# Moving the z loads of a fused FFT convolution and soft MoE to GpSimd, in long runs and two row blocks

## The chip, the cores and the metric

The kernel runs on one core of one Trainium2 chip. The time is the device time of one execution, in microseconds (us). The medians quoted are of all runs of a kernel. Most of these runs are of the state "fast"; one of the changed kernel's four and two of e3_fourbuf's four are labelled slow. A ratio is the mean time of one kernel's fast runs over that of the other's fast runs in the same rounds, so it is not quite the ratio of the medians quoted; a ratio carries a 95% interval. The experiments ran on five chips, where the median of the kernel before was 988 to 995 us, so experiments of different chips are best compared by their ratios.

## The reference

```python
# x: (8, 5696, 128), h: (5696, 128)
Xf, Hf = rfft(x, n=2*S, axis=1), rfft(h, n=2*S, axis=0)
y = irfft(Xf * Hf, n=2*S, axis=1)[:, :S]          # a causal long convolution
x = y.reshape(45568, 128)
logits = x @ phi                                   # 32 slots, 4 for each of 8 experts
d = softmax(logits, axis=0); slot_in = d.T @ x     # over all tokens
slot_out = relu(slot_in @ w1) @ w2                 # per expert
out = softmax(logits, axis=1) @ slot_out
```

## The kernel before

The convolution is a transform in two factors (90 and 64), all as matmuls, and runs as a pipeline over 72 "steps" of 8 to a batch. Stage A transforms columns and stores f to DRAM; stage B loads f, multiplies by the spectrum of h, transforms back and stores z to DRAM; stage C loads z, does the last transform, the logits and both softmaxes. Stage C takes two steps for a *pair* of chunks, and there are four pairs to a batch, 32 in all. The parts that matter:

```python
    def load_z(c):                       # one chunk: 90 rows, 8 KB each
        b, j = divmod(c, NJ)
        t_ = zring.pop(0); zring.append(t_)
        w_ = 2 * CH * 2 * D
        nc.sync.dma_start(out=t_[Z0:Z0 + N1, ...],            # Z0 = 20
                          in_=zd[b].rearrange(...)[:, j * w_:(j + 1) * w_])
    ...
    def stage_c1(T, between):
        za, zb = zs.pop(2 * T), zs.pop(2 * T + 1)
        ...                              # 16 matmuls that read za and zb, PSUM copies, sums
        def after():                     # four GpSimd operations on y, 5.3 us
            ...
    # z store of stage B: three buffers
        st = bpool.tile([P, 2, 2 * D], F32, name="zst", tag="zst", bufs=3)
        nc.scalar.activation(st[:, 0:n, :], bz[:, 0:n, 0:2 * D], AF.Copy)
        nc.sync.dma_start(out=zd[g - 1][...], in_=st[:, 0:n])
    # the loop over steps
        if pair(1 - 2 * ahead) is not None:      # ahead = 1 in the main part, 2 in the tail
            load_pair(pair(1 - 2 * ahead))       # first thing in the step before use
        ...                                      # stages A, B, C
        if U is not None:
            softmax(U)                           # ends with a GpSimd multiply
```

In the main part there is room for one pair of z only: the load of the next pair must wait for the 16 matmuls that read this one, and the next 16 must wait for that load.

Of the kernel before, what the change touches and what calls it, by code (L numbers as in the profile page):

```python
# [10 lines left out]
F32 = mybir.dt.float32  # L11
# [3 lines left out]
PSUM = bass.MemoryType.PSUM  # L15


def transform_tables(S, N1, N2, CH, Z0, X0, F0, F1):












    N, R1, HALF, P = N1 * N2, S // N2, N2 // 2, 2 * N2
    k1 = np.arange(N1)
    alpha = np.pi * (k1 + 0.5) / N1
    m1 = np.arange(R1) - (N1 - 1) / 2
    a1 = np.outer(m1, alpha)
    s1 = np.stack([np.cos(a1), -np.sin(a1), -np.cos(a1)], 1)
    a0 = np.outer(alpha, np.arange(N1 // 2) + 0.5)
    i1 = np.stack([np.cos(a0), -np.sin(a0), -np.cos(a0)], 1)
    NP = N1 // 2
    part = s1  # L40
    s1 = np.zeros((P, 3, P))
    for a, p in enumerate((F0, F1)):
        s1[X0:X0 + R1, :, p:p + NP] = part[:, :, a * NP:(a + 1) * NP]
    i1 = np.pad(i1[np.arange(N1).reshape(2, N1 // 2).T.reshape(-1)],
                [(Z0, P - N1 - Z0), (0, 0), (0, N2 - N1 // 2)])
    k2 = np.arange(N2)
    omega = np.pi * (k1[:, None] + 2 * N1 * k2[None] + 0.5) / N
    m2 = np.arange(HALF) - (N2 - 1) / 2
    a2 = m2[None, :, None] * omega[:, None, :]
    w = np.concatenate([np.cos(a2), np.sin(a2)], 1)  # L50
    back = np.arange(N2).reshape(2, HALF // CH, CH).transpose(1, 0, 2).reshape(-1)
    NU = (NP + 1) // 2
    turn = (N1 - 1) / 2 * alpha[:, None] + (N2 - 1) / 2 * omega
    wq = np.zeros((2, N2, NP, N2))
    vq = np.zeros((2, N2, NU, 2, N2))
    tn = np.zeros((2, N2, 2, NU, 2))
    for a in range(2):
        wq[a] = w[a * NP:(a + 1) * NP].transpose(1, 0, 2)
        for q in range(NP):
            vq[q % 2, :, q // 2, a] = w[a * NP + q][back].T  # L60
            tn[q % 2, :, 0, q // 2, a] = np.cos(turn[a * NP + q]) / N
            tn[q % 2, :, 1, q // 2, a] = np.sin(turn[a * NP + q]) / N
    wq, vq, tn = [t.reshape(P, *t.shape[2:]) for t in (wq, vq, tn)]
    return [np.ascontiguousarray(t, dtype=np.float32) for t in (s1, i1, wq, vq, tn)]
# [3 lines left out]
def kernel(  # L68
# [24 lines left out]
    nc = tc.nc  # L93
    P = 128
    B, S, D = x.shape
# [4 lines left out]
    N1, N2 = 90, 64  # L100
    R1, HALF, NP = S // N2, N2 // 2, N1 // 2
    CH = 4
    NJ = HALF // CH
# [4 lines left out]
    HP = P // 2  # L108
    NQ = NJ // 2
    assert S == R1 * N2 and R1 == N1 - 1 and D == P and CH == Q == 4  # L110
    SPLIT = R1 // 16 * 16
    Z0, X0, F0, F1 = 20, 20, 6, 82
    ctx.enter_context(tc.manual_schedule())

    t_s1, t_i1, t_w, t_v, t_turn = [
        nc.inline_tensor(t, f"tab_{n}").ap()
        for n, t in zip(("s1", "i1", "w", "v", "turn"), transform_tables(S, N1, N2, CH, Z0, X0, F0, F1))]
    fd = [nc.dram_tensor(f"f_{g}", (2, N2, NP, 2, D), F32, kind="Internal").ap() for g in range(B + 1)]
    zd = [nc.dram_tensor(f"z_{b}", (NP, 2 * N2, 2, D), F32, kind="Internal").ap() for b in range(B)]
    cd = nc.dram_tensor("c_t", (P, B * NQ, Q, 2, MH), F32, kind="Internal").ap()  # L120
# [7 lines left out]
    i1 = const.tile([P, 3, HP], F32, name="i1")  # L128
    acc = const.tile([P, D + 1], F32, name="acc")
    NT = B * NQ  # L130
# [12 lines left out]
    ypool = work.enter_context(tc.tile_pool(name="ypool", bufs=1))  # L143
# [7 lines left out]
    bpool = front.enter_context(tc.tile_pool(name="bpool", bufs=1))  # L151

    s1 = apool.tile([P, 3, P], F32, name="s1", tag="s1", bufs=1)
    wt = fconst.tile([P, NP, HP], F32, name="wt")
    vt = fconst.tile([P, NU, 2, HP], F32, name="vt")
    turn = fconst.tile([P, 2, NU, 2], F32, name="turn")
# [110 lines left out]
    def stage_b2(u):  # L267
        g, i = divmod(u, NU)
        if g == 0:
            return  # L270
        n = min(2, NP - 2 * i)
        y_ = prods.pop(u)
        bz = bps.tile([P, 2, 512], F32, name="bz", tag="bz")
        for q in range(n):
            r = slice(q * HP, (q + 1) * HP)
            for a in range(2):
                nc.tensor.matmul(bz[a * HP:(a + 1) * HP, q, 0:2 * D], vt[r, i, a, :],  # L277
                                 y_[r, a, :, :].rearrange("p c d -> p (c d)"),
                                 start=True, stop=True)
        st = bpool.tile([P, 2, 2 * D], F32, name="zst", tag="zst", bufs=3)  # L280
        nc.scalar.activation(st[:, 0:n, :], bz[:, 0:n, 0:2 * D], AF.Copy)  # L281
        nc.sync.dma_start(
            out=zd[g - 1][2 * i:2 * i + n, :, :, :].rearrange("q r c d -> r q (c d)"),
            in_=st[:, 0:n, :])
# [2 lines left out]

    zs, ys, Ls, ds = {}, {}, {}, {}
    ybufs = [ypool.tile([P, Q * CH, D + 1], F32, name=f"y{i}") for i in range(2)]
    zring = [ypool.tile([P, 2, CH, 2, D], F32, name=f"zc{i}") for i in range(2)]  # L290
    lt = ypool.tile([P, CH, 2, HP], F32, name="lt")
    dt = ypool.tile([P, CH, 2, HP], F32, name="dt")
    om, op = [ypool.tile([P, CH, D], F32, name=n) for n in ("om", "op")]
    yt = ypool.tile([D, Q * CH, 2, MH], F32, name="yt")
    for t_ in zring:
        nc.vector.memset(t_[:, :, :, :, :], 0.0)
    for t_ in (lt, dt):
        nc.vector.memset(t_[:, :, :, :], 0.0)
    for t_ in ybufs:
        nc.vector.memset(t_[:, :, D:D + 1], 1.0)  # L300

    def load_z(c):
        b, j = divmod(c, NJ)
        t_ = zring.pop(0)
        zring.append(t_)
        w_ = 2 * CH * 2 * D
        nc.sync.dma_start(
            out=t_[Z0:Z0 + N1, :, :, :, :].rearrange("k o n c d -> k (o n c d)"),
            in_=zd[b].rearrange("q (a r) c d -> (q a) (r c d)",
                                a=2)[:, j * w_:(j + 1) * w_])  # L310
        zs[c] = t_

    def load_pair(T):
        if T < NT:
            load_z(2 * T)
            load_z(2 * T + 1)

    def stage_c1(T, between):
        za, zb = zs.pop(2 * T), zs.pop(2 * T + 1)
        y_ = ybufs[T % 2]  # L320

        def part(v, f):
            k = (2 * v + f) * CH
            return y_[:, k:k + CH, 0:D] if f == 0 else y_[:, k + CH - 1:k - 1:-1, 0:D]

        def product(o, tab, q):
            p = bank()
            for h_, t_ in enumerate((za, zb)):
                nc.tensor.matmul(p[h_ * HP:(h_ + 1) * HP, :], i1[:, tab, :], t_[:, o, :, q, :],  # L329
                                 start=True, stop=True)  # L330
            return p[:, :].rearrange("p (n d) -> p n d", d=D)

        def fold_out(even, minus, plus):
            nc.vector.tensor_tensor(out=plus, in0=even, in1=minus, op=AL.add)  # L334
            nc.vector.tensor_tensor(out=minus, in0=even, in1=minus, op=AL.subtract)

        b_, a_ = product(0, 1, 1), product(0, 0, 0)
        nc.scalar.activation(part(0, 0), b_, AF.Copy)  # L338
        fold_out(a_, part(0, 0), part(1, 0))
        between()  # L340
        b_, a_ = product(1, 1, 0), product(1, 2, 1)
        nc.scalar.activation(om[:, :, :], b_, AF.Copy)

        def after():
            fold_out(a_, om[:, :, :], op[:, :, :])
            for v, o_ in ((1, op), (0, om)):
                for part_, sign in ((part(v, 1), AL.subtract), (part(v, 0), AL.add)):
                    nc.gpsimd.tensor_tensor(out=part_, in0=part(v, 0), in1=o_[:, :, :], op=sign)  # L348

        ys[T] = y_  # L350
        return after
# [193 lines left out]
    for t in range(steps):  # L545
        us = list(units(t))

        def pair(lag):
            T, half = divmod(t - LAG_C - lag, 2)
            return T if half == 0 and 0 <= T < NT else None  # L550
# [18 lines left out]
        for tab, src, first, n, k in ((wt, t_w, LAG_B - 2, NP, 2 * PER),  # L569
                                      (vt, t_v, LAG_B + NJ - 2, NU, PER)):  # L570
            p0 = k * (t - first)
            if 0 <= p0 < n:
                v = slice(p0, min(n, p0 + k))
                nc.sync.dma_start(out=tab[:, v], in_=src[:, v])
        if pair(1 - 2 * ahead) is not None:
            load_pair(pair(1 - 2 * ahead))
        if t < NA:
            load_x(t + 3)
            stage_a(t, 0)
# [28 lines left out]
        if U is not None:  # L608
            softmax(U)
            if U == NT - 1:  # L610
                join_quarters()
        if t == NJ:
            prefetch(AHEAD)
        if t == NA:
# [5 lines left out]
        if t == last_front:  # L620
            front.close()
            rings.append(mid.enter_context(tc.tile_pool(name="ps2", bufs=4, space=PSUM)))
            last = work.enter_context(tc.tile_pool(name="last", bufs=1))
            tail["last"] = last
            tail["cT"] = last.tile([P, B, R1, 2 * NJ], F32, name="cT")
            tail["pool"] = cload.enter_context(tc.tile_pool(name="cload", bufs=3))
            w2s = last.tile([P, E, NFC, D], F32, name="w2s")
            for i in range(2):
                t_ = last.tile([P, 2, CH, 2, D], F32, name=f"zd{i}")
                nc.vector.memset(t_[:, :, :, :, :], 0.0)  # L630
                zring.insert(i, t_)
            assert pair(1) is not None
            load_pair(pair(1) + 2)
            ahead = 2
# [19 lines left out]
    p = bank()  # L654
# [127 lines left out]
```

## Time and profile before

| | before |
|---|---|
| median time | 992.21 us (991.51 to 998.82, 4 runs) |
| span of the profiled run | 980.8 us (this execution took 982.5, less than any of the four timed ones) |
| TensorE, VectorE, ScalarE, GpSimd busy | 88, 68, 52, 47% |
| DMA bytes | 272.79 MB, 278 GB/s over the span |
| period of a pair, 285.47 to 710.96 us | 23.6 us (18 periods) |
| ScalarE waiting for z stores, 190 to 800 us | 67.4 us |

The row of periods is the useful one: cut a steady pipeline at the same instruction of each turn, and the differences say more than busy shares. Below, pairs are numbered from 0 by the start of their first product: pair 0 starts at 192.52 us, pair 4 at 285.47, pair 22 at 710.96, pair 31 at 874.77. (The prediction overlooked pair 0 and counts one less.)

### The profile page before, as it was taken

To read this page: it belongs to the slowest core of one execution; us is meant where nothing else is said; L and a number is where in the kernel's file an instruction comes from. 1 tells how busy PE (TensorE), PEld (TensorE's weight loads), DVE (VectorE), ACT (ScalarE), POOL (GpSimd) and SP (SyncE) were. 2 spreads that over 40 slices of the span, in tenths; PEclk is the share of its full clock that TensorE was granted. 3 is DMA by queue.
4 is the path that set the end of the run, shared out by engine and by line. 5 is a ranking of instruction groups with operands and counts; after the bars stand their busy time and mean duration, and the time that the engine had idled before them with its cause. 6 is when DMAs were issued, how large, how long until landed. Compare 5 with 4: busy or idle time off the path is not lost.

```text
span 980.8 us, 20314 instructions
## 1 busy us (share of the span) xinstructions
PE 862.6 (88%) x7220; PEld 403.2 (41%) x7220; DVE 671.7 (68%) x1137; ACT 510.8 (52%) x1051; POOL 462.4 (47%) x427
## 2 busy tenths in 40 slices
PE   6778788899999999999999999999998887875893
PEld 2222233334444444444444444444443333332883
DVE  2034577568888878777878787777788996554542
ACT  3557545445666655556555565555554443443442
POOL 5546532245555555555555555555533432694000
PEclk9979999999999999999999999999999997797875
DMA  7988899899999998998999899989998996853598
GB/s 193 269 260 266 266 324 327 270 312 295 301 294 313 296 299 276 287 303 261 307 289 297 266 298 287 300 261 288 306 279 264 297 285 190 247 174 122 224 406 328
DMA packets 177283, 272.79 MB, mean 278 GB/s; under 512 B 15024, under 2 KB 119728, under 8 KB 171423
## 3 DMA queue, kind: packets, MB, share of 16 engines
q1 hardware_dynamic: 176607, 271.13, 88.7%
q8 instruction: 58, 0.95, 0.4%
q10 hardware_dynamic: 576, 0.36, 0.2%
q14 instruction: 42, 0.34, 0.1%
HBM read 143.04 MB, written 128.39 MB: 277 GB/s over the span
## 4 chain that ended last, share of the span: by engine, by line
PE 55%; DMA 22%; POOL 7%; DVE 6%; issue 3%; ACT 3%; SPq 2%; DVEq 0%; ACTq 0%; POOLq 0%
PE bank L204 19%; PE bank L329 11%; PE bt L237 9%; DMA z<-zst 8%; PE bz L277 6%; DMA zc<-z 5%; POOL y L348 5%; DMA out_dram<-o 4%; DMA gt<-f 3%; PE bank L357 3%; PE bank L442 2%; PE bank L366 2%; PE bank L395 1%; DVE yf L263 1%; DMA f<-fst 1%
## 5 line engine op out<-in xcount | busy, mean ns | idle before, releaser
L204 PE MATMUL bank<-x,s 128*128 128x512 f32 x576 | 287.3, 626 | 9.5 <-POOL x L193 7.9
L193 POOL TENSOR_TENSOR x<-xc 128x512 f32<-128x512 f32 x144 | 183.4, 1275 | 141.0 <-PE bank L204 124.6
L281 ACT ACTIVATE zst<-bz 128x512 f32<-128x512 f32 (+1 forms) x184 | 108.3, 588 | 222.6 <-PE bz L277 138.5
L206 ACT ACTIVATE fst<-bank 128x512 f32<-128x512 f32 x288 | 168.6, 597 | 86.0 <-PE bank L204 69.0
L258 DVE TENSOR_TENSOR pr<-bt,Hr 128x512 f32<-128x512 f32 (+1 forms) x184 | 126.6, 688 | 81.3 <-PE bt L237 77.2
L237 PE MATMUL bt<-gt,wt 64*64 64x256 f32 x1620 | 138.2, 404 | 37.6 <-PE bz L277 9.9
L263 DVE TENSOR_TENSOR yf<-pr,pi 128x512 f32<-128x512 f32 (+1 forms) x184 | 158.1, 859 | 6.4
L204 PEld LDWEIGHTS bank<-x,s 128*128 128x128 f32 x576 | 100.5, 193 | 132.8 <-issue 89.0
L329 PE MATMUL bank<-zc,i 128*64 128x512 f32 x480 | 137.6, 620 | 17.3 <-ACT y L338 11.4
L261 DVE TENSOR_TENSOR pi<-bt,Hi 128x512 f32<-128x512 f32 (+1 forms) x184 | 125.2, 681 | 0.0
L277 PE MATMUL bz<-yf,vt 64*64 64x256 f32 x1440 | 118.1, 382 | 7.0 <-DVE yf L263 4.5
L237 PEld LDWEIGHTS bt<-gt,wt 64*64 64x64 f32 x1620 | 44.4, 132 | 154.7 <-PE bank L204 52.4
L348 POOL TENSOR_TENSOR y<-y,op 128x512 f32<-128x512 f32 x64 | 75.7, 1183 | 59.2 <-DVE op L334 56.6
L348 POOL TENSOR_TENSOR y<-y,om 128x512 f32<-128x512 f32 x64 | 85.4, 1334 | 2.5
L403 POOL MEMSET dt<- 64x8 f32 x32 | 3.4, 107 | 175.8 <-ACT dn L406 115.3
L277 PEld LDWEIGHTS bz<-yf,vt 64*64 64x64 f32 x1440 | 53.4, 132 | 45.0 <-issue 9.5
L357 PE MATMUL bank<-ident,y 109*128 109x109 f32 x512 | 60.7, 266 | 10.5 <-POOL y L348 10.4
L329 PEld LDWEIGHTS bank<-zc,i 128*64 128x64 f32 x480 | 32.5, 138 | 87.3 <-issue 40.5
L359 ACT ACTIVATE yt<-bank 128x360 f32<-128x360 f32 x128 | 53.0, 471 | 29.3 <-PE bank L357 29.2
L248 DVE SCALAR_TENSOR_TENSOR Hr<-bt,turn,ph 128x128 f32<-128x128 f32 (+1 forms) x46 | 16.0, 349 | 76.0 <-ACT ph L246 76.0
L357 PEld LDWEIGHTS bank<-ident,y 109*128 109x128 f32 x512 | 49.6, 143 | 26.4 <-POOL y L348 17.0
L334 DVE TENSOR_TENSOR y<-bank,y 128x512 f32<-128x512 f32 x32 | 22.1, 690 | 44.9 <-ACT y L338 36.8
(95 smaller groups left out, 911.1 us busy)
## 6 DMA issues: line engine op xcount, KB each, us to landing
f<-fst SPq DMA_DIRECT2D x288, 180.0 KB
gt<-f SPq DMA_DIRECT2D x198, 256.0 KB
z<-zst SPq DMA_DIRECT2D x176, 256.0 KB
zc<-z SPq DMA_DIRECT2D x60, 720.0 KB
xc<-in_x_dram SPq DMA_DIRECT2D x64, 320.0 KB
out_dram<-o SPq DMA_DIRECT2D x16, 1024.0 KB
out_dram<-o SPq DMA_DIRECT2D x8, 768.0 KB
c_t<-cst SPq DMA_DIRECT2D x26, 180.0 KB
```

Of the source, the lines that this page charges most:

```text
L193: nc.gpsimd.tensor_tensor(out=y_[:, :, :], in0=t_[:, 0, :, :], in1=t_[:, 1, ::-1, :], op=AL.subtract if comp else AL.add)
L204: nc.tensor.matmul(p[:, :], s1[:, tab[G], :], src[:, :, :].rearrange("p n d -> p (n d)"), start=True, stop=True)
L206: nc.scalar.activation(st[:, :, G, :], p[:, :].rearrange("p (n d) -> p n d", d=D), AF.Copy)
L237: nc.tensor.matmul(bt[q * HP:(q + 1) * HP, a, 0:2 * D], wt[r, 2 * i + q, :], t_[r, q, :, :].rearrange("p c d -> p (c d)"), start=True, sto ...
L258: nc.vector.tensor_tensor(out=pr[r, :, :, :], in0=pv, in1=Hr[r, i, :, :].unsqueeze(2).broadcast_to([n * HP, 2, 2, D]), op=AL.mult)
L261: nc.vector.tensor_tensor(out=pi[r, :, :, :], in0=pv, in1=Hi[r, i, :, :, :], op=AL.mult)
L263: nc.vector.tensor_tensor(out=y_[r, :, :, :], in0=pr[r, :, :, :], in1=pi[r, :, ::-1, :], op=AL.add)
L277: nc.tensor.matmul(bz[a * HP:(a + 1) * HP, q, 0:2 * D], vt[r, i, a, :], y_[r, a, :, :].rearrange("p c d -> p (c d)"), start=True, stop=True)
L281: nc.scalar.activation(st[:, 0:n, :], bz[:, 0:n, 0:2 * D], AF.Copy)
L329: nc.tensor.matmul(p[h_ * HP:(h_ + 1) * HP, :], i1[:, tab, :], t_[:, o, :, q, :], start=True, stop=True)
L348: nc.gpsimd.tensor_tensor(out=part_, in0=part(v, 0), in1=o_[:, :, :], op=sign)
L357: nc.tensor.transpose(p[:, i * TR:(i + 1) * TR], ys[T][0:TR, k * CH + i, 0:D], ident[0:TR, 0:TR])
```

## The change

The intent is to take the z loads out of SyncE's queue, where stores and loads of the other stages stand behind them, to give them longer runs in two row blocks, and to give the z stores one more buffer. The core of the diff:

```diff
+def z_blocks(n):
+    return [(0, 64, 32), (64, n - 64, 0)]        # rows, count, first partition
...
-        st = bpool.tile([P, 2, 2 * D], F32, name="zst", tag="zst", bufs=3)
+        st = bpool.tile([P, 2, 2 * D], F32, name="zst", tag="zst", bufs=4)
...
-    zring = [ypool.tile([P, 2, CH, 2, D], F32, name=f"zc{i}") for i in range(2)]
+    zring = [ypool.tile([P, 2, 2, CH, 2, D], F32, name="zc")]
...
-    def load_pair(T):
-        if T < NT:
-            load_z(2 * T)
-            load_z(2 * T + 1)
+    def load_pair(T):
+        ...
+        w_ = 2 * 2 * CH * 2 * D
+        for r, n, p in z_blocks(N1):
+            nc.gpsimd.dma_start(
+                out=t_[p:p + n, ...], in_=zd[b].rearrange(...)[r:r + n, j * w_:(j + 1) * w_])
...
-        if pair(1 - 2 * ahead) is not None:      # start of the step before use
-            load_pair(pair(1 - 2 * ahead))
...
             softmax(U)
+        if pair(-2 * ahead) is not None:         # end of the step before that
+            load_pair(pair(-2 * ahead))
```

The table of the last transform gets its rows in the same two blocks. In the changed kernel the lines shift a little: the products L329 are L333, L193 is L200, L281 is L288, L348 is L352, L431 is L435, and the load is L316.

More of the change, by code (lines that the diff above doesn't have):

```diff
@@ L15, with transform_tables @@
 PSUM = bass.MemoryType.PSUM
-def transform_tables(S, N1, N2, CH, Z0, X0, F0, F1):
+def z_blocks(n):
+    return [(0, 64, 32), (64, n - 64, 0)]
+def transform_tables(S, N1, N2, CH, X0, F0, F1):
     N, R1, HALF, P = N1 * N2, S // N2, N2 // 2, 2 * N2
@@ L43, in transform_tables @@
         s1[X0:X0 + R1, :, p:p + NP] = part[:, :, a * NP:(a + 1) * NP]
-    i1 = np.pad(i1[np.arange(N1).reshape(2, N1 // 2).T.reshape(-1)],
-                [(Z0, P - N1 - Z0), (0, 0), (0, N2 - N1 // 2)])
+    part = i1[np.arange(N1).reshape(2, NP).T.reshape(-1)]
+    i1 = np.zeros((P, 3, N2))
+    for r, n, p in z_blocks(N1):
+        i1[p:p + n, :, 0:NP] = part[r:r + n]
     k2 = np.arange(N2)
@@ L111 @@
     SPLIT = R1 // 16 * 16
-    Z0, X0, F0, F1 = 20, 20, 6, 82
+    X0, F0, F1 = 20, 6, 82
     ctx.enter_context(tc.manual_schedule())
@@ L116 @@
         nc.inline_tensor(t, f"tab_{n}").ap()
-        for n, t in zip(("s1", "i1", "w", "v", "turn"), transform_tables(S, N1, N2, CH, Z0, X0, F0, F1))]
+        for n, t in zip(("s1", "i1", "w", "v", "turn"), transform_tables(S, N1, N2, CH, X0, F0, F1))]
     fd = [nc.dram_tensor(f"f_{g}", (2, N2, NP, 2, D), F32, kind="Internal").ap() for g in range(B + 1)]
@@ L294 @@
     yt = ypool.tile([D, Q * CH, 2, MH], F32, name="yt")
-    for t_ in zring:
-        nc.vector.memset(t_[:, :, :, :, :], 0.0)
+    nc.vector.memset(zring[0][:, :, :, :, :, :], 0.0)
     for t_ in (lt, dt):
@@ L300 @@
         nc.vector.memset(t_[:, :, D:D + 1], 1.0)
-    def load_z(c):
-        b, j = divmod(c, NJ)
+    def load_pair(T):
+        if T >= NT:
+            return
+        b, j = divmod(T, NQ)
         t_ = zring.pop(0)
         zring.append(t_)
-        w_ = 2 * CH * 2 * D
-        nc.sync.dma_start(
-            out=t_[Z0:Z0 + N1, :, :, :, :].rearrange("k o n c d -> k (o n c d)"),
-            in_=zd[b].rearrange("q (a r) c d -> (q a) (r c d)",
-                                a=2)[:, j * w_:(j + 1) * w_])
-        zs[c] = t_
-    def load_pair(T):
-        if T < NT:
-            load_z(2 * T)
-            load_z(2 * T + 1)
+        w_ = 2 * 2 * CH * 2 * D
+        for r, n, p in z_blocks(N1):
+            nc.gpsimd.dma_start(
+                out=t_[p:p + n, :, :, :, :, :].rearrange("k h o n c d -> k (h o n c d)"),
+                in_=zd[b].rearrange("q (a r) c d -> (q a) (r c d)",
+                                    a=2)[r:r + n, j * w_:(j + 1) * w_])
+        zs[T] = t_
     def stage_c1(T, between):
-        za, zb = zs.pop(2 * T), zs.pop(2 * T + 1)
+        t_ = zs.pop(T)
         y_ = ybufs[T % 2]
@@ L327, in product @@
             p = bank()
-            for h_, t_ in enumerate((za, zb)):
-                nc.tensor.matmul(p[h_ * HP:(h_ + 1) * HP, :], i1[:, tab, :], t_[:, o, :, q, :],
-                                 start=True, stop=True)
+            for h_ in range(2):
+                nc.tensor.matmul(p[h_ * HP:(h_ + 1) * HP, :], i1[:, tab, :],
+                                 t_[:, h_, o, :, q, :], start=True, stop=True)
             return p[:, :].rearrange("p (n d) -> p n d", d=D)
@@ L627 @@
             w2s = last.tile([P, E, NFC, D], F32, name="w2s")
-            for i in range(2):
-                t_ = last.tile([P, 2, CH, 2, D], F32, name=f"zd{i}")
-                nc.vector.memset(t_[:, :, :, :, :], 0.0)
-                zring.insert(i, t_)
+            t_ = last.tile([P, 2, 2, CH, 2, D], F32, name="zd")
+            nc.vector.memset(t_[:, :, :, :, :, :], 0.0)
+            zring.insert(0, t_)
             assert pair(1) is not None
```

## The prediction

The sum came to -16 us, that is 976 us, but terms of it are cut. In item 1 these are the time of the packets of the 26 rows and the 1.2 us of a pair that all z packets were to save; with the 0.3 us for 2 KB packets, 1.2 takes 23.5 us to 22.0. In item 3 it is how a load came to take 7 us (5 us on the engines and 2 us fixed); added to the 15.7 us to the issue, they make the load chain's 22.6 (22.5 to 22.7). The 7 us, and the 5 us that a load takes in the second rival, were estimates of mine that no trace showed.

> **What bounds the kernel now.** I read the page's slices first, then the table of stretches, then the waits by engine, then the order of time around one step, and last the trace's packet records. Stage C (inverse transform and softmax) runs in pairs of steps; each pair T starts with the products of L329, which read one z load of 1,440 KB (two of 720 KB). Pairs 3 to 22 start at 285.47 to 732.78 us; up to pair 21 (710.96 us) all stages overlap, 425.5 us for 18 periods, 23.6 us each. The slices (PE, then DMA):
>
> ```profile
> PE   6778788899999999999999999999998887875893
> DMA  7988899899999998998999899989998996853598
> ```
>
> Both rows stand at 9 for half the span: two resources are near their limit, so I cut eight pairs at the L329 starts; four of them (us, busy by engine, granted clock, DMA share, GB/s):
>
> ```profile
> 285.47:307.77 22.30, 22.30 (x201) 10.44 (x197) 19.19 (x32) 13.94 (x27) 12.78 (x12) 1.00 1.02 325
> 307.77:331.14 23.37, 22.51 (x200) 10.27 (x196) 19.41 (x32) 13.70 (x27) 12.77 (x12) 1.00 0.99 302
> 400.59:424.88 24.29, 23.58 (x200) 10.45 (x196) 19.39 (x32) 13.71 (x27) 12.76 (x12) 1.00 0.98 287
> 424.88:449.54 24.66, 23.59 (x201) 10.45 (x197) 19.43 (x32) 13.71 (x27) 12.80 (x12) 1.00 1.01 305
> ```
>
> About 200 matmuls take 22.30 us in one pair and 24.66 us in another, at the same clock: PE's busy time stretches with the pair and is no floor. The best pair at hand took 21.6 us (263.88 to 285.47), which I take as TensorE's floor. The DMA share is 1.0 in all four: share times length is 22.7, 23.1, 23.8 and 24.9 us of DMA work. So the transfers set the pace, and PE feels them through two waits. ScalarE's, over 190 to 800 us (total, times, longest):
>
> ```profile
> ACT zst L281 <- DMA z<-zst: 67.4, 19, 5.2
> ```
>
> This is the eviction into a z store buffer that is still being stored; the PSUM copies behind it (L338) come late, and PE waits for those in its second products. And the DMA queue's own:
>
> ```profile
> SPq L282 <- DMA zc<-z: 40.0, 14, 4.7
> SPq L223 <- DMA zc<-z: 33.7, 16, 3.4
> SPq L477 <- DMA zc<-z: 26.6, 14, 3.2
> SPq L307 <- DMA z<-zst: 19.0, 9, 4.2
> ```
>
> The issuer stands still for about 100 us because z loads have not landed, and new stores and loads queue behind 1,440 KB of z. The chain shows the same in one place:
>
> ```profile
> 389.65 0.56 SPq L307
> 390.21 0.05 issue
> 390.26 11.40 DMA zc<-z
> 401.66 0.04 issue
> 401.71 1.93 PE bank L329 x6
> ```
>
> A z load issued 12.4 us into its pair (377.25) landed 24.4 us into it and released the next products.
>
> **Why the z loads are dear.** From the packet records between 285 and 711 us I took the mean time of a packet by size: 1 KB 49.9 ns, 2 KB 105 ns (median 84), 4 KB median 159, but 8 KB 508 (median 522). A line through the medians of 1, 2 and 4 KB gives about 310 ns for 8 KB (an estimate; the few 8 KB packets of the instruction queue have a median of 330). The 8 KB packets are the z loads and hold 24.2% of the 16 engines' time there, 5.7 us of a 23.6 us pair, where 310 ns would need 3.5.
>
> [...]
>
> **The change part by part.** The instruction order of ACT is unchanged, PE's and DVE's too but for two pairs of clearing memsets merged; the 64 z loads leave SyncE, and 64 new ones enter GpSimd's queue behind the softmax multiply L431, one step earlier in the program than before.
>
> 1. DMA work. Before: 180 packets x 508 ns = 91 us of engine time in a pair. After: 64 packets of 16 KB at 2 x 310 = 620 ns[...] 2 KB packets should also lose part of their excess of 21 ns; call it 0.3 us. DMA work of a full pair falls from about 23.5 to 22.0 us: just off the limit.
> 2. SyncE's queue. The zc waits above go; z stores no longer queue behind z loads, and the fourth buffer gives one more store of slack. I expect the ACT wait of 67.4 us to fall below 15. On PE it is worth 0.5 to 1 us of a pair, but it shares that with item 1.
> 3. The new chain. GpSimd reaches the load only after four L348, a fold and L431:
>
> ```profile
> 293.22 2.44 POOL L348 TENSOR_TENSOR y<-y,op 128x512 f32<-128x512 f32 x2 [2.04 <-DVE op L334]
> 295.62 2.90 POOL L348 TENSOR_TENSOR y<-y,om 128x512 f32<-128x512 f32 x2
> 298.48 1.29 POOL L193 TENSOR_TENSOR x<-xc 128x512 f32<-128x512 f32 x1
> 299.71 1.50 POOL L431 TENSOR_TENSOR L<-L,rs 128x512 f32<-128x512 f32 x1
> 301.18 1.27 POOL L193 TENSOR_TENSOR x<-xc 128x512 f32<-128x512 f32 x1
> ```
>
> In this pair (from 285.47) that is 15.7 us after its first product, against 12.4 for SyncE in the example. [...]
> 4. GpSimd itself. [...] At a batch's first pair GpSimd waits for the last z stores, as SyncE did (19 us over nine times), now with folds behind it.
>
> **The sum.** A full pair becomes the largest of TensorE 21.6, DMA 22.0 and the load chain 22.6: 1.0 us gained of 23.6. Pairs 3 to 21: 19 x 1.0 = 19 us; the first three pairs, 23 to 25 us long, 3 more; ScalarE's 5.5 us of z store waits ahead of stage C, 1. Against it the tail: from pair 23 on there is no stage A and a pair takes 19.6 us (751.88, 771.50, 791.09). There L431 ends 5.5 us ahead of the next products (784.50 + 1.04 to 791.09), less than the 7 us of a load, where SyncE issued 10 us ahead: five pairs x 1.5 = 7 us lost. After the last front stage two pair buffers serve and nothing is lost. Net -16 us: 976 us.
>
> **The rivals.**
> - The z load has no priority on the engines[...]. For: it now starts 3 us later, and has one buffer in the main part. Against: packets of 16 KB among those of 1 and 2 KB. At 9 us instead of 7 a pair takes 24.6 and the tail loses 3.5 each: 19 + 17 - 4 = 32 us more, 1,025.
> - Everything lands in time. [...] pairs go to about 21.8 and the tail loses nothing: 22 x 1.8 = 40 us less, 953. For: pairs of 21.6 and 22.3 us exist already. Against: DMA work of 22 us.
> - Hidden anyway: TensorE and DVE (19.2 of 22.3 us) fill what the transfers give up, or the batch boundaries block the folds by 3 us seven times (21 us). Then 985 to 995.
>
> **Range and chances.** The sum is 16 us below, the good rival 40, the bad one 32 above. The good one seems likelier than the bad, since it is fed by shorter queues, shorter packets per byte and a freed issuer. I say 976 us, 950 to 1,003 in eight cases of ten. Two per cent faster is 973: 0.43; within, 0.49; slower, 0.08.
>
> **What will show it.** Right: L431 is followed by two z loads on GpSimd, packets of 16 KB with a mean near 600 to 800 ns; the z loads' share falls from 24% to below 20%; the ACT wait on z<-zst is below 15 us; SyncE waits for no z load; the pairs from 285 to 711 last 22.5 us; pairs 24 to 27 last 21. Wrong: 16 KB packets above 1,000 ns, a DMA share still at 1.0 with z stores waited for, PE waiting for z loads by over 1 us in every pair, or folds (L204 waiting for POOL) on the chain. The whole is wrong if a z load takes 9 us or more from GpSimd's issue to landing.

## The result, and the profile after

The changed kernel takes **1,094.97 us** (1,085.41 to 1,103.54, 4 runs, one of them slow) against 992.21: ratio 1.100, interval 1.090 to 1.110. It is 10% slower. The prediction said 976 us, with a range of 950 to 1,003.

The slices of the changed kernel (PE, granted TensorE clock, DMA), and its two main DMA queues (packets, MB, share of 16 engines):

```profile
PE   6687887888888888898889888888787777676994
PEclk9989899899999999989998999999898999786865
DMA  7988999787889877777887778878875865654298
...
q1 hardware_dynamic: 169887, 223.94, 63.2%
q0 software_dynamic: 4096, 47.19, 14.3%
```

Where DMA and PE both stood at 9, both are now mostly at 8 or 7: neither looks like the limit any more, something makes both wait. Pairs 4, 8 and 9 of the changed kernel, cut at the first product, with the columns of the prediction's table of stretches (PE, PEld, DVE, ACT, POOL busy; clock, DMA share, GB/s):

```profile
304.35:328.57 24.22, 22.60 (x197) 10.46 (x197) 20.07 (x29) 13.91 (x27) 13.77 (x13) 1.00 0.81 261
410.18:439.51 29.33, 25.22 (x196) 11.12 (x197) 21.96 (x31) 14.06 (x27) 13.75 (x13) 0.91 0.73 219
439.51:468.30 28.79, 24.29 (x197) 10.77 (x197) 21.90 (x31) 13.96 (x27) 13.76 (x13) 0.92 0.80 247
```

The DMA share of these three fell from 1.0 to 0.73 to 0.81, while the pairs became longer; over pairs 4 to 21 its mean is 0.80, where the kernel before has 0.96. The waits of TensorE name the cause (us in total, times, longest):

```profile
PE bank L333 <- DMA zc<-z: 75.6, 28, 5.6
PE bz L284 <- DVE yf L270: 25.3, 26, 1.2
```

Nearly every one of the 32 pairs waits for its z load; in the kernel before that wait was 5.7 us in all (the weight loads of these products waited 17.2 us more, and 9.3 in the changed kernel). The second line has another cause: once in each of 22 pairs VectorE's L270 takes 1.9 to 3.5 us, 3.2 in the mean, in place of 0.7 to 1.4, while GpSimd is at the issue of the load and the fold behind it. TensorE loses about 1 us by it, but between the issue and the landing of the load, and it waits for the load afterwards (in pair 8 0.95 us at 432.75, then 3.16 at 439.51), so this is not on the path. Why VectorE is held up was not tested. With the loads issued by SyncE, or early, it doesn't occur.

Pair 8 in order of time, first GpSimd and then TensorE (start, length, what, idle time before it and what ended it):

```profile
420.55 2.44 POOL L352 TENSOR_TENSOR y<-y,op 128x512 f32<-128x512 f32 x2 [3.03 <-DVE op L338]
422.96 2.89 POOL L352 TENSOR_TENSOR y<-y,om 128x512 f32<-128x512 f32 x2
425.81 1.28 POOL L200 TENSOR_TENSOR x<-xc 128x512 f32<-128x512 f32 x1
427.04 1.51 POOL L435 TENSOR_TENSOR L<-L,rs 128x512 f32<-128x512 f32 x1
428.49 1.04 POOL L316 DMA_DIRECT2D zc<-z  x2
429.54 2.50 POOL L200 TENSOR_TENSOR x<-xc 128x512 f32<-128x512 f32 x2
```

```profile
405.68 0.61 PE L284 MATMUL bz<-yf,vt 64*64 64x256 f32 x8
410.18 3.68 PE L333 MATMUL bank<-zc,i 128*64 128x512 f32 x8 [3.90 <-DMA zc<-z]
414.84 2.36 PE L333 MATMUL bank<-zc,i 128*64 128x512 f32 x8
439.51 1.06 PE L333 MATMUL bank<-zc,i 128*64 128x512 f32 x2 [3.16 <-DMA zc<-z]
```

The first product of pair 8 runs at 410.18. GpSimd issues the next load at 428.49, 18.3 us later, and pair 9 starts at 439.51, 11.0 us after the issue. The two add up to the period of 29.3 us, and because pair 9 waits for that load (3.16 us), the two together set the period. Over pairs 4 to 22 the means are:

| | issue of the next load after the first product | from issue to the next first product | period |
|---|---|---|---|
| before | 13.4 us | 10.2 us | 23.6 us |
| changed | 17.1 us | 10.5 us | 27.6 us |

The same chain is there in both kernels. The load takes about as long as before; it starts 3.7 us later. (In the kernel before the first product needs only the first of two chunks, so I also took the time from the issue to the end of the last z packet: 10.0 us before, 9.6 changed.)

The two profiled spans differ by 117.3 us. Pair 0 starts 8.4 us later (200.88 for 192.52), pairs 0 to 4 take 10.5 us more (103.5 for 93.0), the 18 periods to pair 22 take 71.8 more (497.3 for 425.5), pairs 22 to 31 take 26.6 more (190.4 for 163.8), and the end the same 106 us. The loss is spread over the whole of stage C. (The medians differ by 102.8 us; the profiled run of the kernel before was a fast one.)

One more line of the trace was unexpected: the first eight products took 3.68 us in pair 8, and 1.94 in pair 4. The stretches around 410 us, same columns as above:

```profile
404.00:408.00 4.00, 2.29 (x19) 0.71 (x18) 3.92 (x7) 1.79 (x4) 1.27 (x1) 1.00 0.97 260
408.00:410.00 2.00, 0.00 (x0) 0.00 (x0) 0.77 (x2) 0.00 (x0) 0.00 (x0) 0.73 0.99 350
411.00:412.00 1.00, 1.00 (x6) 0.34 (x4) 0.00 (x0) 0.00 (x0) 0.00 (x0) 0.50 0.87 255
416.00:420.00 4.00, 4.00 (x30) 1.72 (x26) 2.44 (x5) 2.17 (x6) 1.16 (x2) 1.00 0.27 98
```

The granted clock falls to 0.50 during the wait, at 408.9 us, and stays there until 415.7. In the clock records of this trace there are 15 such spells between 304 and 801 us, from pair 4 to pair 21, all at 0.50 and each 3.41 or 6.83 us long. Fifteen of the 18 pairs 4 to 21 have slow first products (the first eight take 3.0 to 3.7 us); these issue the next load 16.8 to 18.3 us into the pair, the three others at 15.7. A wait of the array thus costs more than its length here. The length of the wait alone does not decide: first products were slow after a recorded wait of 2.0 us (pair at 354.15) and not after one of 2.7 (at 304.35).

### The profile page after: what moved, and what is told of

It reads as the page before. It is cut to its first block, busy times and chain, and to the rows that moved or that the text cites. A ratio compares the mean times of both kernels' runs of the same rounds, so it can differ in the third digit from the quotient of the medians.

```text
span 1098.1 us, 20427 instructions
## 1 busy us (share of the span) xinstructions
PE 899.8 (82%) x7220; PEld 415.8 (38%) x7220; DVE 730.1 (66%) x1135; ACT 516.6 (47%) x1051; POOL 494.6 (45%) x491
## 3 DMA queue, kind: packets, MB, share of 16 engines
q0 software_dynamic: 4096, 47.19, 14.3%
## 5 line engine op out<-in xcount | busy, mean ns | idle before, releaser
L200 POOL TENSOR_TENSOR x<-xc 128x512 f32<-128x512 f32 x144 | 183.0, 1279 | 142.8 <-issue 74.6
L333 PE MATMUL bank<-zc,i 128*64 128x512 f32 x480 | 155.1, 777 | 75.6 <-DMA zc<-z 75.6
L270 DVE TENSOR_TENSOR yf<-pr,pi 128x512 f32<-128x512 f32 (+1 forms) x184 | 202.4, 1100 | 6.4
L288 ACT ACTIVATE zst<-bz 128x512 f32<-128x512 f32 (+1 forms) x184 | 108.3, 588 | 191.4 <-PE bz L284 181.4
L352 POOL TENSOR_TENSOR y<-y,op 128x512 f32<-128x512 f32 x64 | 75.8, 1184 | 80.0 <-DVE op L338 77.5
L333 PEld LDWEIGHTS bank<-zc,i 128*64 128x64 f32 x480 | 38.5, 163 | 143.2 <-issue 131.6
L352 POOL TENSOR_TENSOR y<-y,om 128x512 f32<-128x512 f32 x64 | 85.5, 1335 | 2.5
L361 PE MATMUL bank<-ident,y 109*128 109x109 f32 x512 | 62.5, 270 | 13.5 <-POOL y L352 13.4
L342 ACT ACTIVATE y<-bank 128x512 f32<-128x512 f32 x32 | 19.1, 598 | 106.6 <-PE bank L333 106.6
```

What stands on the lines that cost most here:

```text
L200: nc.gpsimd.tensor_tensor(out=y_[:, :, :], in0=t_[:, 0, :, :], in1=t_[:, 1, ::-1, :], op=AL.subtract if comp else AL.add)
L270: nc.vector.tensor_tensor(out=y_[r, :, :, :], in0=pr[r, :, :, :], in1=pi[r, :, ::-1, :], op=AL.add)
L333: nc.tensor.matmul(p[h_ * HP:(h_ + 1) * HP, :], i1[:, tab, :], t_[:, h_, o, :, q, :], start=True, stop=True)
L352: nc.gpsimd.tensor_tensor(out=part_, in0=part(v, 0), in1=o_[:, :, :], op=sign)
L361: nc.tensor.transpose(p[:, i * TR:(i + 1) * TR], ys[T][0:TR, k * CH + i, 0:D], ident[0:TR, 0:TR])
```

## The experiments

The theories. **Late**: the load is issued too late because it stands in GpSimd's queue behind four y operations, a fold and a multiply (in pair 8 these run from 420.55 us on, and the issue follows at 428.49). **GpSimd**: the software queue itself, the q0 of the page (4,096 packets, 14.3% of the engines), costs the time. **Layout**: long runs and two unequal blocks cost the engines more than they save.

All results together; "period" is the mean of the 18 periods of pairs 4 to 22 in the profiled run.

| run | what | median us | ratio to before (95%) | period us |
|---|---|---|---|---|
| changed | GpSimd, late place, blocks | 1,094.97 | 1.100 (1.090 to 1.110) | 27.6 |
| e1_sync | SyncE, old place, blocks | 971.19 | 0.979 (0.974 to 0.984) | 22.8 |
| e2_early | GpSimd, early, blocks | 992.51 | 1.001 (0.996 to 1.007) | 23.5 |
| e3_fourbuf | before, four store buffers | 992.21 | no ratio given, two runs fast | 23.9 |
| e4_syncearly | SyncE, early, blocks | 954.19 | 0.963 (0.959 to 0.966) | 22.3 |
| e5_syncplace | SyncE, changed place, blocks | 976.65 | 0.982 (0.976 to 0.988) | 23.0 |
| e6_oldlayout_early | SyncE, early, two loads of 90 rows | 978.22 | 0.981 (0.975 to 0.987) | 23.1 |
| e7_run90 | SyncE, old place, one load of 90 rows | 995.69 | 1.003 (0.997 to 1.009) | 24.1 |
| e8_eightports | as e1, other partitions | 1,012.55 | 1.020 (1.011 to 1.030) | 24.1 |
| e9_mixed | GpSimd early, SyncE for first pairs | 960.48 | 0.966 (0.961 to 0.970) | 22.4 |
| e10_gpsplit | GpSimd early, 64 rows always early | 976.53 | 0.984 (0.975 to 0.992) | 23.0 |
| e11_syncsplit | the same by SyncE | 969.96 | 0.977 (0.967 to 0.987) | 23.1 |
| e12_warm | changed, 12 idle matmuls | 1,103.56 | 1.116 (1.111 to 1.120) | 27.3 |
| e13_warm6 | changed, 6 idle matmuls | 1,065.54 | 1.071 (1.064 to 1.077) | 25.9 |

All gave correct results.

### e1_sync: give the loads back to SyncE

```diff
-            nc.gpsimd.dma_start(
+            nc.sync.dma_start(
...
+        if pair(1 - 2 * ahead) is not None:
+            load_pair(pair(1 - 2 * ahead))       # the place of the kernel before
...
-        if pair(-2 * ahead) is not None:
-            load_pair(pair(-2 * ahead))
```

> The changed kernel, but its z loads (same 16 KB runs, same blocks of 64 and 26 rows, four z store buffers) issued by SyncE at the place of the kernel before. Theory 'late' (the load starts about 17 us into the pair because it stands behind GpSimd's four y operations, and the next products wait for it): SyncE issues about 12 us into the pair, the lateness goes, time 970 to 995 us, and PE's waits for z loads fall from 76 us to below 15. Theory 'GpSimd' (the software queue itself[...] costs the time wherever it starts): also 970 to 995. Theory 'layout' (long runs and unequal blocks cost the engines more than they save): above 1,030 us, and 16 KB packets again near 880 ns.

Measured 971 us, 2.1% faster than before: the layout is not at fault, it helps. The mean of all 16 KB packets is again 880 ns, as foreseen for the theory "layout", but the time is not, and this theory falls. "Late" and "GpSimd" both stand.

### e2_early: let GpSimd issue earlier

```diff
             after = stage_c1(T, rows)
+            if ahead == 2 or (T + 1) % NQ:       # not the first pair of a batch
+                load_pair(T + ahead)
...
-        if pair(-2 * ahead) is not None:
-            load_pair(pair(-2 * ahead))
+        if T is not None and ahead == 1 and (T + 1) % NQ == 0:
+            load_pair(T + 1)                     # first pair of a batch: must wait for z stores
+        if t == LAG_C - 2:
+            load_pair(0)
```

> The changed kernel, but GpSimd issues the next pair's load right behind the products that read the buffer, ahead of its four y operations, about 7 us into the pair instead of 17; only the first pair of a batch, which must wait for the last z stores, keeps its place. Theory 'late': the load lands about 18 us into the pair, pairs of 22 to 23 us, 955 to 985 us. Theory 'GpSimd': the queue costs as much at 7 us as at 17, above 1,060 us, and the waits move to the folds or to DVE. Theory 'layout': above 1,030.

Measured 992.5 us: 102 us less than the changed kernel, with the same queue, packets and blocks. GpSimd's queue in this run:

```profile
318.63 1.05 POOL L415 TENSOR_TENSOR L<-L,rm 128x512 f32<-128x512 f32 x1 [0.78 <-DVE rm L414]
319.63 1.04 POOL L316 DMA_DIRECT2D zc<-z  x2
321.73 2.45 POOL L352 TENSOR_TENSOR y<-y,op 128x512 f32<-128x512 f32 x2 [1.05 <-DVE op L338]
```

The issue now stands ahead of L352, 5.6 us into most pairs, and most of those have a period of 22.3 us: the load is off their path. The first pairs of the batches, which kept the late place, issue at 15.2 us and, up to pair 20, are followed 24.9 to 27.4 us after the pair ahead of them. TensorE's wait for z loads fell from 75.6 us to what these leave:

```profile
PE bank L333 <- DMA zc<-z: 24.1, 8, 5.6
```

The time missed the expected 955 to 985 of "late" from above, and was far below the 1,060 of "GpSimd".

### e3_fourbuf: the fourth store buffer alone

```diff
-        st = bpool.tile([P, 2, 2 * D], F32, name="zst", tag="zst", bufs=3)
+        st = bpool.tile([P, 2, 2 * D], F32, name="zst", tag="zst", bufs=4)
```

> The kernel before with four z store buffers in place of three, nothing else. If the ScalarE wait for z stores is what SyncE's queue costs, it falls from 67 us to below 20 and the time by 5 to 15 us; if the transfers set the pace, the wait moves to z loads and the time stays within 0.5%.

No gain is shown: the median is 992.21 us against 990.27 for before on the same chip, but only two of the four runs are fast, and these took 992.05 and 977.57 us. By these a gain of up to 1.3% is not excluded; but e7 below has four buffers too and is no faster than before (1.003). In the profiled run, of 992.05 us, the wait moved. ScalarE's wait for z stores (190 to 800 us) fell from 67.4 us to

```profile
ACT zst L281 <- DMA z<-zst: 6.4, 5, 1.5
```

and the weight loads of the products now wait for z loads over the whole run, 37.1 us where the kernel before had 17.2:

```profile
PEld bank L329 <- DMA zc<-z: 37.1, 24, 3.0
```

### e4_syncearly: early, by SyncE

The edit is that of e2_early with `nc.sync.dma_start` for the load.

> As the run before last (early loads), but issued by SyncE. Theory 'late': as good as GpSimd early, 955 to 985 us, the two within 1% of each other. Theory 'GpSimd': this one is 955 to 985 and GpSimd early is above 1,060. Theory 'layout': both above 1,030.

Measured 954.19 us, 3.75% faster than before: the best. Two stretches of 22 us in the steady part, columns as above, and TensorE's wait for z loads between 190 and 850 us:

```profile
283.00:305.00 22.00, 22.00 (x198) 10.44 (x196) 18.89 (x32) 13.66 (x28) 12.78 (x11) 1.00 0.97 302
305.00:327.00 22.00, 22.00 (x198) 10.45 (x196) 18.89 (x31) 13.71 (x27) 12.77 (x11) 1.00 0.97 306
```

```profile
PE bank L333 <- DMA zc<-z: 2.2, 2, 1.4
```

A pair now lasts 22.3 us in the mean, and TensorE is busy throughout both stretches; the four pairs of the kernel before in the prediction's table took 22.3 to 24.7. GpSimd early is 38 us behind, not within 1%, so something of GpSimd's remained to be explained.

### e5_syncplace: only the issuer changed back

One word of the changed kernel: `nc.sync` for `nc.gpsimd` in the load, at its place at the end of the step.

> The changed kernel with one word changed: the z loads stay at the changed kernel's place in the program (the end of the step before), but SyncE issues them. If it is GpSimd's own order of work (four y operations, a fold and a multiply ahead of the load) that makes them late, SyncE issues 10 to 13 us into the pair and the time is 965 to 980 us, as with SyncE at the old place. If the place in the program is at fault, it is late here too and the time stays above 1,050 us.

Measured 976.65 us, with the issue 10.4 to 13.4 us into the pair. Pair 8 of this run, SyncE and then TensorE:

```profile
391.23 2.25 SPq L316 DMA_DIRECT2D zc<-z  x2
```

```profile
380.86 1.94 PE L333 MATMUL bank<-zc,i 128*64 128x512 f32 x8
404.26 1.94 PE L333 MATMUL bank<-zc,i 128*64 128x512 f32 x8 [1.03 <-DMA zc<-z]
```

The place in the program is not late in itself. The same line is 118 us apart in the two queues, because SyncE has nothing ahead of it but issues, and GpSimd has 8 us of work that itself waits for the pair's products. Once issued, the load is no slower from GpSimd: from the issue to the end of its last packet it takes 9.6 us in the changed kernel, 9.8 here and 9.6 in e1 (means of 18 loads).

### e6_oldlayout_early and e7_run90: what the layout is worth

e6 is e4 with the load of the kernel before (two loads of 90 rows of 8 KB at partition 20); e7 is e1 with `z_blocks` returning `[(0, n, 20)]`, one load of 90 rows of 16 KB.

> Early loads by SyncE, four z store buffers, but the layout of the kernel before: two loads of 90 rows of 8 KB at partition 20. Theory 'lateness is all': as fast as the early SyncE kernel with the new layout, 950 to 960 us. Theory 'the layout also pays by relieving the engines': pairs of 22.8 to 23.5 us in place of 22.3, 965 to 985 us.

> SyncE at the old place, four z store buffers, one load of 90 rows of 16 KB at partition 20. It separates the long run from the two blocks. If the blocks[...] make the gain, this has packets of about 2 x 510 = 1,020 ns and takes 985 to 995 us, as the kernel before; if the long run or the single issue makes it, 965 to 978 us as with blocks.

e6: 978.22 us, so the blocks with their long runs are worth 24 us by the medians when nothing is late, and 18 by the ratios (0.981 against 0.963; e4 and e6 ran on different chips). e7: 995.69 us, no faster than before: long runs without the blocks give nothing. From the packet records of each run from 290 to 700 us:

| z packets | mean ns | median ns | GB/s in a packet |
|---|---|---|---|
| before, 8 KB, 90 rows at 20 | 509 | 522 | 16 |
| e7, 16 KB, 90 rows at 20 | 1,052 | 1,112 | 16 |
| e1, 16 KB, 64 rows at 32, 26 at 0 | 877 | 734 | 19 |
| changed, the same from GpSimd (300 to 780 us) | 891 | 829 | 18 |
| e8, 16 KB, 64 rows at 0, 26 at 64 | 1,181 | 1,221 | 14 |

### e8_eightports: the same blocks on other partitions

```diff
-    return [(0, 64, 32), (64, n - 64, 0)]
+    return [(0, 64, 0), (64, n - 64, 64)]
```

> SyncE at the old place, new blocks (971 us), but the 64 rows stand at partitions 0 to 63 and the 26 at 64 to 89. [...] the 64-row packets go from about 730 ns to about 1,250 and the mean of all from 880 to 1,250 or so, and the time rises to 985 to 1,010 us. If partitions don't matter, mean 880 ns and 965 to 978 us.

Measured 1,012.55 us, 41 us above e1, with nothing changed but the partitions: the packets take 1,181 ns in place of 877. What the run shows is that the partitions in which the rows land change the time of a packet, not why. That the kernel before is slow for the same reason, in a milder form, is likely (e7 against e1) but not shown by a run of its own.

### e9_mixed: the first pairs by SyncE

The edit gives `load_pair` an issuer and passes `nc.sync` in the two late calls of e2_early.

> GpSimd early (992 us) with the seven loads of a batch's first pair and the very first load given to SyncE. If what GpSimd still costs against SyncE (38 us) lies only in those first pairs, where its load stands 15 us into the pair (periods of 25 instead of 22.3), the time falls to 952 to 962 us. If the software queue costs time everywhere, it stays above 975.

Measured 960.48 us. By moving eight of 32 loads 32 of the 38 us came back. The remaining 6 us (ratio 0.966 against 0.963, with overlapping intervals) are all that GpSimd's software queue could cost by itself in the other 24 loads, as they stand here: early and with time to spare. That it costs nothing on the path either is read from the durations under e5.

### e10_gpsplit and e11_syncsplit: the 64 rows always early

```diff
-            if ahead == 2 or (T + 1) % NQ:
-                load_pair(T + ahead)
+            load_pair(T + ahead, (0, 1) if ahead == 2 or (T + 1) % NQ else (0,))
...
-            load_pair(T + 1)
+            load_pair(T + 1, (1,))               # only the 26 rows wait for the last z stores
```

> GpSimd early (992 us), and for the first pair of a batch the 64-row block, whose z stores are long done, is issued early as well; only the 26 rows wait for the last stores at the old place. The late part is then 416 KB in place of 1,440. If first pairs are long because 1,440 KB start 15 us into the pair, their period falls from 25 to about 22.5 to 23.5 us and the time to 962 to 978 us. If they are long because GpSimd stands still there, it stays above 985.

> The same by SyncE, against 954 us with the whole load late in first pairs. First pairs there are at 22 to 23.6 us already, so 950 to 956 us: within 0.5%, at best a little faster.

GpSimd: 976.53 us, as expected; those first pairs follow after 22.6 to 25.0 us in place of 24.9 to 27.4. SyncE: 969.96 us, a miss: 16 us slower than with the whole load late (1.4% by the ratios). The DMA queue's waits show SyncE standing at the load for z stores for

```profile
SPq L319 <- DMA z<-zst: 48.1, 15, 6.8
```

where e4 had 15.5 us over 11 times. The longer standstill may be the cause, but no run tests it. Why the 64 rows wait for stores at all was not followed up.

### e12_warm and e13_warm6: keep TensorE's clock up

```diff
-        def product(o, tab, q):
+        def product(o, tab, q, warm=0):
             p = bank()
+            for _ in range(warm):
+                nc.tensor.matmul(p[0:HP, 0:3 * HP], i1[:, tab, :],
+                                 i1[:, :, :].rearrange("p t c -> p (t c)"), start=True, stop=True)
...
-        b_, a_ = product(0, 1, 1), product(0, 0, 0)
+        b_, a_ = product(0, 1, 1, 12), product(0, 0, 0)       # e13: 6
```

> The changed kernel with twelve idle matmuls (64 x 192, about 2.2 us, their result is overwritten) ahead of each pair's first products, where TensorE waits 3 to 4 us for the z load and afterwards runs at a granted clock of 0.50. If the half clock lengthens the chain (first products 3.6 us in place of 1.94, and L435 ends 17.4 us into the pair in place of 15.7), the load is issued about 1.7 us earlier, pairs go from 27.6 to about 25.5 us, and the time from 1,095 to 1,035 to 1,060 us. If the half clock is hidden in the chain, the time stays within 1% of 1,095.

With twelve: 1,103.56 us, a miss. The clock stayed up (mean 0.952 over the span, 0.901 in the changed kernel) and the issue came forward from 17.1 to 15.8 us, but the idle matmuls took 4.1 us instead of 2.2 (an estimate: eight records of 512 columns take 1.94 us in pair 4, so the 24 of 192 columns that the twelve leave 2.2), overran the landing, and the products followed 11.4 us after the issue instead of 10.5. The run gave no answer.

> The changed kernel with six idle matmuls (about 2.05 us by the run before) ahead of each pair's first products. If the half clock lengthens the chain, the issue comes 15.8 us into the pair as with twelve, the products follow 10.0 to 10.5 us later as in the changed kernel, pairs take 26.0 to 26.4 us in place of 27.6, and the time falls to 1,050 to 1,075 us. If what the clock gives is taken back in the load, it stays within 1% of 1,095.

With six: 1,065.54 us; issue at 15.6 us, products 10.3 us later, period 25.9 us. About 30 of the 103 us between the changed kernel and the one before come from the half clock (mean clock 0.954 in place of 0.901, first products at 1.94 to 2.2 us in all pairs but one): it slows the first products after the wait, which puts off the y operations, which puts off the next load. That is a loop, not a single cost.

## Why the prediction was wrong

**Right.** The DMA work did fall: the z loads' share went from 24.2% of a 23.6 us pair (5.7 us) to 18.0% of 27.4 us between 300 and 780 us (4.9 us). All DMA work of a pair, share times length, fell from 22.8 to 22.2 us, where the sum had 23.5 to 22.0. SyncE waits for no z load any more, and ScalarE's wait for z stores fell to 1.0 us. The estimate of the packets, a mean of 600 to 800 ns, was near: it is 891 ns. TensorE's floor, taken as 21.6 us, is near: e4's pairs 4 to 21 take 21.6 to 23.6 us, 22.3 in the mean.

**Wrong: step 3, "the new chain", in its size.** It said 15.7 us to the issue and 7 us to the products, together 22.6, just below the old 23.6. Measured are 17.1 and 10.5, together 27.6. Term by term:

- *To the issue*, +1.4 us. The 15.7 came from one pair without a wait. During most waits for z TensorE's granted clock falls to 0.50 (15 of 18 pairs), which lengthens the way to the next issue (16.8 to 18.3 us against 15.7); with the clock kept up it is 15.6 us (e13). No step of the prediction had this.
- *From issue to the first packet*, 1.6 us (mean of 18 loads), *and after the last packet*, 0.9 us: 2.5 for the 2 us that I had added (an estimate without a trace).
- *On the engines*, 8.0 us for 5.0. The packets were not the miss: 90 of 891 ns make 5.0 us on 16 engines. But while a load runs, z packets hold 63% of the engines' time and the packets of the other queue 35%: the load got two thirds of the engines, where I had counted on nearly all of them without a trace that showed it.

**And in its choice.** Step 3 saw that the load would start 3 us later than SyncE's and set its 7 us, an estimate for a transfer served nearly alone that no trace showed, into a pair of which only 6 us were left (21.6 less 15.7). The old load, in the same trace, took 11.4 us on loaded engines in the very lines that were quoted. Taking that duration instead of 7 gives 15.7 + 11.4 = 27.1 us, near the measured 27.6. The first rival, a load without priority on the engines, went the right way (63% measured) and stopped at 9 us, 1,025 us in all. The prediction's last sign of being wrong, 9 us or more from the issue to landing, is what came: 10.4 us in the mean (by the page, medians of 7.8 us for the 1,024 KB block and 9.3 for the 416 KB block).

**What the runs show in its place.** GpSimd's order of work is the cause, by where the load stands in it. The same load moved up by 10 us in that queue gains 102 us (e2), SyncE at the same place in the program gains 118 (e5), and the load itself takes no longer from GpSimd than from SyncE (9.6 us against 9.6 to 9.8, e1 and e5). With early loads, the software queue costs at most about 6 us (e9). Of the 103 us between the two medians about 30 come through the half clock (e13). The change carries one good part, the two blocks: about 18 to 24 us (e4 against e6, and e1 against e7), which the late issue buried.

**Left open.** Why splitting the load slows SyncE by 16 us (e11), whether GpSimd's last 6 us are real, why VectorE's L270 is held up beside GpSimd's issue, and why a packet's time depends on its partitions (e8).

## What to carry to other kernels

With a single buffer, a load is part of the loop: add up *from first use to issue* and *from issue to landing*, with the landing time measured under load, before moving it to another queue. An engine that also computes issued its load only when its earlier work was done (17.1 us into the pair, and 5.6 when moved up); put the load right behind the last reader of its buffer. If a transfer is slow per byte, look first at which partitions its rows land in before lengthening the runs: here 16 KB packets took 877 ns with 64 rows at partition 32 and 26 at 0 (e1), 1,181 with the same blocks at 0 and 64 (e8), and 1,052 with 90 rows at 20 (e7).
